# Attention output transposed by the DMA queue and added in the eviction, with the second token-mixing product row-tiled for two pairs at a time

## The chip, the cores and the metric

The kernel runs on one core of a Trainium2 chip. The metric is the device time of one execution in microseconds (us). Ratios are the mean time of one kernel's fast runs over the mean of the other's fast runs of the same rounds, with a 95% interval, so they are not quite the ratio of the medians that stand beside them. The change and the two groups of experiments (e1 to e4, e5 to e8) ran in separate rounds, so across them the ratios compare better than the medians.

## The reference, cut to what matters

```python
# B=8 batches, H=12 heads, S=448 rows, D=64; C=H*D=768; R=32; F=4*C
q_n, k_n = q / |q|, k / |k|                      # per row
attn = softmax(q_n @ k_n.T / tau)
x    = (attn @ v) -> [B, S, C]                   # heads side by side
h    = x.T @ U @ V                               # token mixing: U [S,R], V [R,S]
u    = x + h.T
out  = u + relu(u @ w_ch1) @ w_ch2               # channel mixing
```

Almost all arithmetic is in the two channel products. Attention and token mixing are done for two heads at a time (a "pair"; six pairs to a batch, 48 in all).

## The kernel before

For each pair, the attention output X (rows in four chunks of 128, 128 columns for two heads) is needed transposed, because the channel product contracts over columns. The kernel accumulates the transposed X (a product with the identity) and the low-rank term A V (A = X^T U, so the sum is u^T) in one PSUM bank, and then casts the bank to bf16.

```python
def step_A(b, p):                      # runs on PE and ScalarE
    X = X_of[(b, p)]
    ap = av_of[(b, p)][:, 384:512]
    for c in range(4):                 # A^T: U is 32 columns, padded to 128 with zeros
        nc.tensor.matmul(out=ap, lhsT=U_sb[:, c, :], rhs=X[:, c, :],
                         start=False, stop=(c == 3), skip_group_check=True)
    A = work.tile([128, 128], BF, name="A_sb", tag="A_sb", bufs=2)
    nc.scalar.copy(out=A, in_=ap)
    ...                                # [cut] up = one PSUM bank
    for c in range(4):                 # the transposed X, by the identity
        n = 128 if c < 3 else 64
        nc.tensor.matmul(out=up[:, c * 128:c * 128 + n], lhsT=X[:, c, :], rhs=ident[:, 0:n],
                         start=(c == 0), stop=False, skip_group_check=True)

def step_H(b, p):                      # the second product, 32 useful rows of 128
    nc.tensor.matmul(out=up, lhsT=A_of[(b, p)], rhs=V_sb,
                     start=False, stop=True, skip_group_check=True)
    ...
    nc.vector.tensor_copy(out=u_of(b)[:, p, 0:S], in_=up)
```

The channel products of the previous batch are a list of steps of about 1 us of PE work each (`fill`), which are dealt out between the attention steps of the current batch. From the third batch on, Q and K are transposed by the DMA queue (SP issues it) already. The weights are loaded early on GpSimd's own queue: `load_w1` in four parts, then `load_w2` in four.

Of the kernel before, what the change touches and what calls it, by code (L numbers as in the profile page):

```python
# [9 lines left out]
FP = mybir.dt.float32  # L10
BF = mybir.dt.bfloat16
# [11 lines left out]
def kernel(  # L23
# [16 lines left out]
    nc = tc.nc  # L40

    B, H, S, D = q.shape
    C = H * D
    R = moe_U.shape[-1]
    F = moe_w_ch1.shape[-1]
    NP = H // 2
# [5 lines left out]
    const = ctx.enter_context(tc.tile_pool(name="const", bufs=1))  # L52
    work = ctx.enter_context(tc.tile_pool(name="work", bufs=2))
    psum = ctx.enter_context(tc.tile_pool(name="psum", bufs=1, space=bass.MemoryType.PSUM))
# [29 lines left out]
    est = Estimate()  # L84
# [23 lines left out]
    for i in range(2):  # L108
        t = const.tile([128, 7, 512], BF, name=f"E{i}")
        nc.gpsimd.memset(t[:, :, S:512], 1.0)  # L110
        E.append(t)

    U_sb = const.tile([128, 4, 128], BF, name="U_sb")
    U_raw = const.tile([128, 4, R], FP, name="U_raw")
    V_raw = const.tile([R, S], FP, name="V_raw")
    V_sb = const.tile([128, S], BF, name="V_sb")
    w1_sb = const.tile([128, CC, F], BF, name="w1_sb")
    w2_sb = const.tile([128, NC, C], BF, name="w2_sb")
    uE = const.tile([128, CC, S], BF, name="uE")
# [3 lines left out]
    def load_mixer():  # L123
        nc.gpsimd.memset(U_sb, 0.0)
        nc.gpsimd.memset(V_sb, 0.0)
        nc.gpsimd.memset(U_raw[64:128, 3, :], 0.0)
        nc.gpsimd.dma_start(out=V_raw, in_=moe_V)
        nc.gpsimd.dma_start(out=U_raw[0:64, :, :], in_=moe_U[0:256].rearrange("(p c) r -> p c r", c=4))
        nc.gpsimd.dma_start(out=U_raw[64:128, 0:3, :], in_=moe_U[256:448].rearrange("(p c) r -> p c r", c=3))

    def place_mixer():
        lo = V_raw[:, 0:256].rearrange("r (p c) -> r c p", c=4)
        hi = V_raw[:, 256:448].rearrange("r (p c) -> r c p", c=3)
        body = V_sb[0:R, 0:384].rearrange("r (c p) -> r c p", p=128)
        nc.scalar.copy(out=U_sb[:, :, 0:R], in_=U_raw)
        nc.scalar.copy(out=body[:, :, 0:64], in_=lo[:, 0:3, :])
        nc.scalar.copy(out=body[:, :, 64:128], in_=hi)
        nc.scalar.copy(out=V_sb[0:R, 384:448], in_=lo[:, 3, :])

    def load_w1(f0, f1):  # L140
        nc.gpsimd.dma_start(out=w1_sb[:, :, f0:f1],
# [115 lines left out]
    def by_dma(n):  # L257

        return n >= 2 * NP
# [40 lines left out]
            est.pe(0.25)  # L300
            est.act(0.93)

    X_of, av_of, A_of, up_of = {}, {}, {}, {}

    def step_V(b, p, half):
        gi, j = group_of[(b, p)]
        vv = norm[gi][1]
        e = E[(b * NP + p) % 2]
        if half == 0:
            X_of[(b, p)] = work.tile([128, 4, 128], BF, name="X", tag="X", bufs=2)  # L310
        X = X_of[(b, p)]
        if b == 0 and half == 1:
            bank = psum.tile([128, 512], FP, name="mp", tag="ps_m", bufs=2)
        else:
            bank = psum.tile([128, 512], FP, name="av", tag="ps_av", bufs=1)
        av_of[(b, p)] = bank
        av = bank[:, 0:4 * (D + 1)].rearrange("p (i h d) -> p i h d", i=2, h=2)
        for i in range(2):
            ic = 2 * half + i
            nc.tensor.matmul(out=av[:, i, :, :], lhsT=e[:, 6, ic * 128:(ic + 1) * 128],  # L320
                             rhs=vv[:, 2 * j:2 * j + 2, 3, :],
                             start=(i == 0), stop=False, skip_group_check=True)
        for i in range(2):
            ic = 2 * half + i
            for h in range(2):
                for c in range(3):
                    nc.tensor.matmul(out=av[:, i, h, :],  # L327
                                     lhsT=e[:, 2 * c + h, ic * 128:(ic + 1) * 128],
                                     rhs=vv[:, 2 * j + h, c, :],
                                     start=False, stop=(i == 1 and h == 1 and c == 2),  # L330
                                     skip_group_check=True)
        rd = work.tile([128, 4, 1], FP, name="rd", tag="rd", bufs=4)
        nc.vector.reciprocal(out=rd, in_=av.rearrange("p i h d -> p (i h) d")[:, :, D:D + 1])  # L333
        nc.vector.tensor_mul(  # L334
            X[:, 2 * half:2 * half + 2, :].rearrange("p i (h d) -> p i h d", h=2),
            av[:, :, :, 0:D],
            rd.rearrange("p (i h) o -> p i h o", h=2).to_broadcast([128, 2, 2, D]))
        est.pe(0.52)
        est.dve(0.6)


    def u_of(b):
        return uE if b % 2 == 0 else uO

    def step_A(b, p):
        X = X_of[(b, p)]
        ap = av_of[(b, p)][:, 384:512]
        for c in range(4):
            nc.tensor.matmul(out=ap, lhsT=U_sb[:, c, :], rhs=X[:, c, :],  # L349
                             start=False, stop=(c == 3), skip_group_check=True)  # L350
        A = work.tile([128, 128], BF, name="A_sb", tag="A_sb", bufs=2)
        nc.scalar.copy(out=A, in_=ap)  # L352
        A_of[(b, p)] = A
        est.pe(0.44)
        est.act(0.3)
        if b == 0:
            up = psum.tile([128, S], FP, name="mp", tag="ps_m", bufs=2)
        else:
            up = psum.tile([128, S], FP, name="up", tag="ps_x", bufs=1)
        up_of[(b, p)] = up  # L360
        for c in range(4):
# [4 lines that stand above are left out]
    def step_H(b, p):  # L366
        up = up_of[(b, p)]
        nc.tensor.matmul(out=up, lhsT=A_of[(b, p)], rhs=V_sb,  # L368
                         start=False, stop=True, skip_group_check=True)
        est.pe(0.19)  # L370
        if b == 0:
            nc.scalar.copy(out=u_of(b)[:, p, 0:S], in_=up)
        else:
            nc.vector.tensor_copy(out=u_of(b)[:, p, 0:S], in_=up)  # L374
            est.dve(0.62)
        if b % 2 == 1 and p == NP - 1:
            nc.vector.tensor_copy(out=uO[:, :, S:512], in_=uE[:, :, 384:S])


# [77 lines left out]
    fill = []  # L457
# [3 lines left out]
    def f(n):  # L461
        for _ in range(n):
            fill.pop(0)()
# [21 lines left out]
    def T(n):  # L485
        step_T(*pairs[n])

    def Sc(n, *cs):
        step_S(*pairs[n], cs)

    def V(n, half):
        step_V(*pairs[n], half)

    def A(n):
        step_A(*pairs[n])

    def Hs(n):
        step_H(*pairs[n])
# [126 lines left out]
    def put(n, at, fn):  # L625
        after.setdefault((n, at), []).append(fn)
# [21 lines left out]
            put(m - 1, -1, lambda m=m: T(m))  # L648
            put(m - 1, 3, lambda m=m: T(m + 1))

    for n in range(NP, NPAIR + 1):
        b, p = pairs[n] if n < NPAIR else (B, 0)
        now, nxt = n < NPAIR, n + 1 < NPAIR
        done = n > NP
        for g in after.pop((n, -1), []):
            g()
        if n % 2 == 0:

            order = [
                (2, now and done and (lambda: Sc(n, 0, 1))),  # L660
                (2, done and (lambda: V(n - 1, 0))),
                (2, now and (lambda: Sc(n, 3))),
                (2, nxt and not by_dma(n + 1) and (lambda: T(n + 1))),
                (2, done and (lambda: V(n - 1, 1))),
                (1, done and (lambda: A(n - 1))),
                (1, nxt and (lambda: (Sc(n, 2), Sc(n + 1, 0)))),
                (1, done and (lambda: Hs(n - 1))),
            ]
        else:
            order = [  # L670
                (2, lambda: Sc(n, 1, 2)),
                (2, lambda: V(n - 1, 0)),
                (2, lambda: Sc(n, 3)),
                (2, lambda: V(n - 1, 1)),
                (2, nxt and not by_dma(n + 1) and (lambda: T(n + 1))),
                (2, lambda: A(n - 1)),
                (1, lambda: Hs(n - 1)),
            ]
        weights = [w if fn else 0 for w, fn in order]
        last = p == 0 and done  # L680
        left = NP - p + 0.85 if not last else 0.85
        nf = len(fill) if last else int(round(len(fill) / left))
        given = acc = 0
        for i, ((_, fn), w) in enumerate(zip(order, weights)):
            if fn:
                fn()
            for g in after.pop((n, i), []):
                g()
            acc += w
            want = nf * acc // sum(weights)  # L690
            f(min(want - given, len(fill)))
            given = want
        if last:
            f(len(fill))
            fill.extend(steps_m1(b - 1) + steps_m2(b - 1))
    f(len(fill))
    assert not after

# [34 lines left out]
```

## Time and profile before

| | before |
|---|---|
| time, median of 4 runs | 618.05 us (617.51 to 618.66) |
| span of the profiled run | 616.0 us |
| PE busy | 589.5 us (96%) |
| VectorE, ScalarE, GpSimd busy | 41%, 46%, 31% |

Busy shares are averages. What decides is whether PE ever waits, and the prediction below reads that from the list of PE's waits and its timeline. In the views PE is TensorE (matmuls) and PEld its weight loads, DVE is VectorE, ACT ScalarE, POOL GpSimd, and SP the engine that issues most DMAs; a bank is one part of PSUM, the memory that the matmuls write here, and to evict it is to copy it to SBUF, where the matmuls' operands lie. PEclk is the granted clock in tenths. Lines such as `302.76 0.36 PE L363 MATMUL ...` give start, duration, engine, source line, operation, tile written and tiles read, shape and count; what stands in brackets is the idle time just before and what ended it. Source lines of the changed kernel are numbered differently: L387, L414 become L439, L466 (channel products), L368 becomes L385 (second mixing product of the first two batches), L297 becomes L312 (row-tiled scores).

### The profile page before, as it was taken

The numbers are of one execution on the slowest core, as the hardware profiler recorded it, in microseconds if no ns is written. First come the engines' busy times: TensorE is split into PE (matmuls) and PEld (weight loads), VectorE is DVE, ScalarE is ACT, GpSimd is POOL, SyncE is SP. The second block draws the span as 40 slices with busy tenths as digits, with TensorE's granted clock in tenths as the row PEclk, the third lists the DMA queues.
The fourth block names the chain that finished last, engine by engine and source line by source line (L and its number), as shares of the span: only waits on it lengthen the run. The fifth ranks groups of instructions, "written<-read, shape, count | busy, mean of one in ns | idle before, by whom it ended". The sixth has DMA issues, their size and how long they took to land.

```text
span 616.0 us, 11649 instructions
## 1 busy us (share of the span) xinstructions
PE 589.5 (96%) x4872; PEld 346.3 (56%) x4872; DVE 249.5 (41%) x478; ACT 284.3 (46%) x519; POOL 190.2 (31%) x155
## 2 busy tenths in 40 slices
PE   1769999999999999999999999999999999999997
PEld 0445556655665555655566556565566555665564
DVE  5763665525325435335244454354352552110000
ACT  5775444455334555355442554354533455314310
POOL 7746274224044054043141351340431410000000
PEclk9998999999999999999999999999999999999999
DMA  7999995662074650562055641373135310110012
GB/s 187 214 230 223 233 216 133 173 150 36 10 166 116 151 125 1 138 167 52 7 134 134 160 100 39 63 174 91 35 95 99 69 24 12 27 37 17 1 51 53
DMA packets 89365, 63.80 MB, mean 104 GB/s; under 512 B 43120, under 2 KB 85664, under 8 KB 89312
## 3 DMA queue, kind: packets, MB, share of 16 engines
q1 hardware_dynamic: 82320, 52.60, 36.0%
q0 software_dynamic: 6688, 10.24, 9.2%
q8 instruction: 38, 0.62, 0.4%
q10 hardware_dynamic: 304, 0.21, 0.1%
q14 instruction: 15, 0.12, 0.1%
HBM read 52.02 MB, written 11.01 MB: 102 GB/s over the span
## 4 chain that ended last, share of the span: by engine, by line
PE 87%; DMA 8%; SPq 2%; POOL 1%; DVE 1%; ACT 1%; issue 0%; POOLq 0%; ACTq 0%
PE mp L414 36%; PE mp L387 32%; PE av L327 5%; PE sc L297 5%; DMA kst<-in_k_dram 5%; DMA vst<-in_v_dram 3%; PE av L320 2%; PE av L349 2%; PE mp L423 2%; PE up L363 1%; PE up L368 1%; PE sc L289 1%; POOL sq L215 1%; DMA qst<-in_q_dram 1%; SPq L182 1%; DVE ss L220 0%
## 5 line engine op out<-in xcount | busy, mean ns | idle before, releaser
L414 PE MATMUL mp<-w_sb,relu 128*128 128x384 bf16 x1344 | 245.1, 326 | 0.0
L414 PEld LDWEIGHTS <-relu 128*128 128x128 bf16 x1344 | 123.5, 98 | 84.8 <-issue 12.2
L387 PEld LDWEIGHTS <-w_sb 128*128 128x128 bf16 x1152 | 106.4, 98 | 100.9 <-issue 11.7
L244 POOL TENSOR_TENSOR qk<-kst,inv 128x512 bf16<-128x512 f32 x47 | 58.1, 1257 | 288.7 <-DVE rd L333 147.8
L391 ACT ACTIVATE relu<-mp 128x448 bf16<-128x448 f32 x155 | 84.2, 543 | 120.0 <-PE mp L387 119.9
L299 ACT ACTIVATE E<-sc 128x896 bf16<-128x896 f32 x144 | 124.6, 918 | 23.7 <-PE sc L297 23.7
L387 PE MATMUL mp<-uE,w_sb 128*128 128x448 bf16 x576 | 121.8, 353 | 0.0
L387 PE MATMUL mp<-uO,w_sb 128*128 128x448 bf16 x576 | 117.1, 353 | 0.0
L428 ACT COPY o_sb<-mp 128x384 f32<-128x384 f32 x55 | 26.3, 478 | 103.5 <-PE mp L423 102.9
L333 DVE RECIPROCAL rd<-av 128x4 f32<-128x4 f32 x90 | 15.6, 174 | 119.8 <-PE av L327 119.7
L244 DVE TENSOR_TENSOR qk<-qst,inv 128x512 bf16<-128x512 f32 x48 | 62.3, 1327 | 0.1
L220 DVE TENSOR_REDUCE ss<-sq 128x16 f32<-128x1024 f32 (+1 forms) x50 | 58.4, 1168 | 7.3 <-POOL sq L215 6.3
L215 POOL TENSOR_TENSOR sq<-kst 128x1024 f32<-128x1024 f32 x21 | 47.3, 2253 | 18.6 <-DMA kst<-in_k_dram 14.6
L327 PE MATMUL av<-v,E 128*128 128x65 bf16 x1080 | 49.4, 195 | 0.0
L297 PE MATMUL sc<-qkT 64*128 64x448 bf16 x288 | 42.0, 367 | 5.5 <-DVE qkT L276 3.6
L327 PEld LDWEIGHTS <-E 128*128 128x128 bf16 x1152 | 46.6, 99 | 0.0
L215 POOL TENSOR_TENSOR sq<-qst 128x1024 f32<-128x1024 f32 x23 | 45.7, 1987 | 2.6 <-DMA vst<-in_v_dram 2.6
L393 DVE TENSOR_SCALAR relu<-mp 128x448 bf16<-128x448 f32 x37 | 23.1, 623 | 49.2 <-PE mp L387 49.2
L334 DVE TENSOR_TENSOR X<-av,rd 128x256 bf16<-128x256 f32 x90 | 38.2, 425 | 3.1
L291 ACT ACTIVATE E<-sc 128x448 bf16<-128x448 f32 x48 | 26.1, 543 | 22.1 <-PE sc L289 22.1
L374 DVE CAST uO<-up 128x448 bf16<-128x448 f32 x24 | 14.9, 621 | 47.4 <-PE up L368 47.4
L352 ACT CAST A_sb<-av 128x128 bf16<-128x128 f32 x42 | 11.1, 263 | 40.4 <-PE av L349 40.4
(78 smaller groups left out, 332.8 us busy)
## 6 DMA issues: line engine op xcount, KB each, us to landing
out_dram<-o_sb SPq DMA_DIRECT2D x54, 192.0 KB, 2.7
w_sb<-in_moe_w_ch_dram POOLq DMA_DIRECT2D x8, 1152.0 KB, 18.6
qst<-in_q_dram SPq DMA_DIRECT2D x23, 256.0 KB, 4.1
vst<-in_v_dram SPq DMA_DIRECT2D x46, 128.0 KB, 2.9
kst<-in_k_dram SPq DMA_DIRECT2D x44, 128.0 KB, 3.7
qst<-in_q_dram SPq DMA_DIRECT2D x23, 192.0 KB, 4.6
vst<-in_v_dram SPq DMA_DIRECT2D x46, 96.0 KB, 2.7
kst<-in_k_dram SPq DMA_DIRECT2D x44, 96.0 KB, 3.4
```

Source lines behind the costliest of these rows:

```text
L215: nc.gpsimd.tensor_mul(sq[:, 0:self.nh * 4, :], self.flat(t), self.flat(t))
L220: nc.vector.reduce_sum(self.ss[:, j, 0:self.nh * 4], self.sq[j][:, 0:self.nh * 4, :], axis=AX.X)
L244: eng.tensor_mul(qks[self.s][:, j, i, :, :, :], t[:, 2 * j:2 * j + 2, :, :].rearrange("p h c d -> p c h d"), iv.unsqueeze(3).to_broadcast( ...
L291: nc.scalar.activation(out=e[:, 6, 0:S], in_=sc[:, 0, 0:S], func=AF.Exp)
L297: nc.tensor.matmul(out=sc[:, h, 0:S], lhsT=t[r, 1, c * 128:(c + 1) * 128], rhs=t[r, 0, 0:S], start=True, stop=True)
L299: nc.scalar.activation(out=e[:, 2 * c:2 * c + 2, 0:S], in_=sc[:, :, 0:S], func=AF.Exp)
L327: nc.tensor.matmul(out=av[:, i, h, :], lhsT=e[:, 2 * c + h, ic * 128:(ic + 1) * 128], rhs=vv[:, 2 * j + h, c, :], start=False, stop=(i == ...
L334: nc.vector.tensor_mul(X[:, 2 * half:2 * half + 2, :].rearrange("p i (h d) -> p i h d", h=2), av[:, :, :, 0:D], rd.rearrange("p (i h) o -> ...
L387: nc.tensor.matmul(out=mp, lhsT=w1_sb[:, cc, f * 128:(f + 1) * 128], rhs=u[:, cc, 0:S], start=(cc == 0), stop=(cc == CC - 1))
L391: nc.scalar.activation(out=relu[:, f, o:o + S], in_=mp, func=AF.Relu)
L414: nc.tensor.matmul(out=mp, lhsT=relu[:, f, r0:r0 + 128], rhs=w2_sb[:, f, half * HC:(half + 1) * HC], start=(f == 0), stop=False, skip_grou ...
L428: nc.scalar.copy(out=o[:, cols], in_=mp)
```

## The change

Intent: from the third batch on, take the identity products off PE. A DMA transpose makes X^T in SBUF, and the vector engine adds it while it evicts the low-rank term. The second product has only 32 useful rows, so two pairs share the array: one on rows 0 to 63, the other on rows 64 to 127. That needs a second copy of U's columns and V's rows at 64 to 95.

```diff
-    V_raw = const.tile([R, S], FP, name="V_raw")
+    V_raw = work.tile([128, S], FP, name="V_raw", tag="XT", bufs=2)
+    A_sb = [const.tile([128, 128], BF, name=f"A_sb{i}") for i in range(2)]
...
+    def load_twin():
+        nc.gpsimd.dma_start(out=V_raw[64:64 + R, :], in_=moe_V)
+
+    def place_twin():
+        nc.gpsimd.tensor_copy(out=U_sb[:, :, 64:64 + R], in_=U_raw)
+        place_v(nc.gpsimd.tensor_copy, 64)          # three copies into V_sb[64:96]
...
+    def step_XT(b, p):
+        t = work.tile([128, 4, 128], BF, name="XT", tag="XT", bufs=2)
+        XT_of[(b, p)] = t
+        nc.sync.dma_start_transpose(out=t, in_=X_of[(b, p)].rearrange("p c d -> p (c d)"))
+
+    def step_A2(b, p):                              # no identity products
+        ...
+        rows = slice(64 * (p % 2), 64 * (p % 2) + 64)
+        nc.scalar.copy(out=A_of[(b, p)][rows, :], in_=ap[rows, :])
+
+    def step_H2(b, p):                              # a couple: pairs p and p + 1
+        ups = (psum.tile([128, 512], FP, name="av", tag="ps_av", bufs=1),
+               psum.tile([128, 512], FP, name="up", tag="ps_x", bufs=1))
+        for i in range(2):
+            rows = slice(64 * i, 64 * i + 64)
+            nc.tensor.matmul(out=ups[i][:, 0:S], lhsT=A_of[(b, p)][rows, :], rhs=V_sb[rows, :],
+                             start=True, stop=True)
+        for i in range(2):
+            xt = XT_of.pop((b, p + i)).rearrange("p c r -> p (c r)")
+            nc.vector.tensor_add(u_of(b)[:, p + i, 0:S], ups[i][:, 0:S], xt[:, 0:S])
...
+    put(NP, 4, load_twin)          # seventh pair
+    put(NP + 2, 0, place_twin)     # ninth pair
...
-                (2, now and done and (lambda: Sc(n, 0, 1))),
+                    (2, lambda: Sc(n, 0, 1)),
...                                  # late pairs: couple behind a score block, then two fill steps
+        Sc(n, 1, 2)
+        if n - 3 >= FIRST2:
+            H2(n - 3)
+        ...
+        f(2)
+        spread(n, order, nf - 2, 1)
```

The cuts leave out the rearranged order of the late pairs and the smaller edits.

More of the change, by code (lines that the diff above doesn't have):

```diff
@@ L111 @@
         E.append(t)
+    U_raw = const.tile([128, 4, R], FP, name="U_raw")
     U_sb = const.tile([128, 4, 128], BF, name="U_sb")
-    U_raw = const.tile([128, 4, R], FP, name="U_raw")
-    V_raw = const.tile([R, S], FP, name="V_raw")
+    V_raw = work.tile([128, S], FP, name="V_raw", tag="XT", bufs=2)
+    A_sb = [const.tile([128, 128], BF, name=f"A_sb{i}") for i in range(2)]
     V_sb = const.tile([128, S], BF, name="V_sb")
@@ L125, in load_mixer, with place_v @@
         nc.gpsimd.memset(V_sb, 0.0)
+        for t in A_sb:
+            nc.gpsimd.memset(t[64:128, :], 0.0)
         nc.gpsimd.memset(U_raw[64:128, 3, :], 0.0)
-        nc.gpsimd.dma_start(out=V_raw, in_=moe_V)
+        nc.gpsimd.dma_start(out=V_raw[0:R, :], in_=moe_V)
         nc.gpsimd.dma_start(out=U_raw[0:64, :, :], in_=moe_U[0:256].rearrange("(p c) r -> p c r", c=4))
         nc.gpsimd.dma_start(out=U_raw[64:128, 0:3, :], in_=moe_U[256:448].rearrange("(p c) r -> p c r", c=3))
+    def place_v(copy, r0):
+        rows = slice(r0, r0 + R)
+        lo = V_raw[rows, 0:256].rearrange("r (p c) -> r c p", c=4)
+        hi = V_raw[rows, 256:448].rearrange("r (p c) -> r c p", c=3)
+        body = V_sb[rows, 0:384].rearrange("r (c p) -> r c p", p=128)
+        copy(out=body[:, :, 0:64], in_=lo[:, 0:3, :])
+        copy(out=body[:, :, 64:128], in_=hi)
+        copy(out=V_sb[rows, 384:448], in_=lo[:, 3, :])
     def place_mixer():
-        lo = V_raw[:, 0:256].rearrange("r (p c) -> r c p", c=4)
-        hi = V_raw[:, 256:448].rearrange("r (p c) -> r c p", c=3)
-        body = V_sb[0:R, 0:384].rearrange("r (c p) -> r c p", p=128)
         nc.scalar.copy(out=U_sb[:, :, 0:R], in_=U_raw)
-        nc.scalar.copy(out=body[:, :, 0:64], in_=lo[:, 0:3, :])
-        nc.scalar.copy(out=body[:, :, 64:128], in_=hi)
-        nc.scalar.copy(out=V_sb[0:R, 384:448], in_=lo[:, 3, :])
+        place_v(nc.scalar.copy, 0)
+    def load_twin():
[3 more added lines that the diff above has]
+        place_v(nc.gpsimd.tensor_copy, 64)
     def load_w1(f0, f1):
@@ L301, in step_S @@
             est.act(0.93)
-    X_of, av_of, A_of, up_of = {}, {}, {}, {}
+    X_of, av_of, A_of, up_of, XT_of = {}, {}, {}, {}, {}
     def step_V(b, p, half):
@@ L313, in step_V @@
             bank = psum.tile([128, 512], FP, name="mp", tag="ps_m", bufs=2)
+        elif half == 1 and by_dma(b * NP + p):
+            bank = psum.tile([128, 512], FP, name="up", tag="ps_x", bufs=1)
         else:
@@ L350, in step_A @@
                              start=False, stop=(c == 3), skip_group_check=True)
-        A = work.tile([128, 128], BF, name="A_sb", tag="A_sb", bufs=2)
-        nc.scalar.copy(out=A, in_=ap)
+        A = A_sb[p % 2]
+        nc.scalar.copy(out=A[0:64, :], in_=ap[0:64, :])
         A_of[(b, p)] = A
@@ L376, in step_H @@
         if b % 2 == 1 and p == NP - 1:
+            nc.vector.tensor_copy(out=uO[:, :, S:512], in_=uE[:, :, 384:S])
+    def step_XT(b, p):
[3 more added lines that the diff above has]
+    def step_A2(b, p):
+        X = X_of[(b, p)]
+        ap = av_of[(b, p)][:, 384:512]
+        for c in range(4):
+            nc.tensor.matmul(out=ap, lhsT=U_sb[:, c, :], rhs=X[:, c, :],
+                             start=False, stop=(c == 3), skip_group_check=True)
+        if p % 2 == 0:
+            A_of[(b, p)] = A_of[(b, p + 1)] = A_sb[(p // 2) % 2]
+        rows = slice(64 * (p % 2), 64 * (p % 2) + 64)
+        nc.scalar.copy(out=A_of[(b, p)][rows, :], in_=ap[rows, :])
+        est.pe(0.22)
+        est.act(0.3)
+    def step_H2(b, p):
[5 more added lines that the diff above has]
+                             start=True, stop=True)
+        est.pe(0.19)
+        for i in range(2):
+            xt = XT_of.pop((b, p + i)).rearrange("p c r -> p (c r)")
+            nc.vector.tensor_add(u_of(b)[:, p + i, 0:S], ups[i][:, 0:S], xt[:, 0:S])
+            est.dve(0.62)
+        if b % 2 == 1 and p == NP - 2:
             nc.vector.tensor_copy(out=uO[:, :, S:512], in_=uE[:, :, 384:S])
@@ L649, with spread @@
             put(m - 1, 3, lambda m=m: T(m + 1))
-    for n in range(NP, NPAIR + 1):
-        b, p = pairs[n] if n < NPAIR else (B, 0)
-        now, nxt = n < NPAIR, n + 1 < NPAIR
-        done = n > NP
-        for g in after.pop((n, -1), []):
-            g()
-        if n % 2 == 0:
-            order = [
-                (2, now and done and (lambda: Sc(n, 0, 1))),
-                (2, done and (lambda: V(n - 1, 0))),
-                (2, now and (lambda: Sc(n, 3))),
-                (2, nxt and not by_dma(n + 1) and (lambda: T(n + 1))),
-                (2, done and (lambda: V(n - 1, 1))),
-                (1, done and (lambda: A(n - 1))),
-                (1, nxt and (lambda: (Sc(n, 2), Sc(n + 1, 0)))),
-                (1, done and (lambda: Hs(n - 1))),
-            ]
-        else:
-            order = [
-                (2, lambda: Sc(n, 1, 2)),
-                (2, lambda: V(n - 1, 0)),
-                (2, lambda: Sc(n, 3)),
-                (2, lambda: V(n - 1, 1)),
-                (2, nxt and not by_dma(n + 1) and (lambda: T(n + 1))),
-                (2, lambda: A(n - 1)),
-                (1, lambda: Hs(n - 1)),
-            ]
-        weights = [w if fn else 0 for w, fn in order]
-        last = p == 0 and done
-        left = NP - p + 0.85 if not last else 0.85
-        nf = len(fill) if last else int(round(len(fill) / left))
+    put(NP, 4, load_twin)
+    put(NP + 2, 0, place_twin)
+    def spread(n, order, nf, first=0):
+        weights = [w if fn is not False else 0 for w, fn in order]
         given = acc = 0
@@ L686 @@
                 fn()
-            for g in after.pop((n, i), []):
+            for g in after.pop((n, i + first), []):
                 g()
@@ L692, with X2, A2, H2 @@
             given = want
-        if last:
+    FIRST2 = 2 * NP
+    KEEP = 3
+    for n in range(NP, NPAIR + 1):
+        b, p = pairs[n] if n < NPAIR else (B, 0)
+        now, nxt = n < NPAIR, n + 1 < NPAIR
+        done = n > NP
+        late = n > FIRST2
+        for g in after.pop((n, -1), []):
+            g()
+        if not late:
+            if n % 2 == 0:
+                order = [
+                    (2, lambda: Sc(n, 0, 1)),
+                    (2, done and (lambda: V(n - 1, 0))),
+                    (2, lambda: Sc(n, 3)),
+                    (2, not by_dma(n + 1) and (lambda: T(n + 1))),
+                    (2, done and (lambda: V(n - 1, 1))),
+                    (1, done and (lambda: A(n - 1))),
+                    (1, lambda: (Sc(n, 2), Sc(n + 1, 0))),
+                    (1, done and (lambda: Hs(n - 1))),
+                ]
+            else:
+                order = [
+                    (2, lambda: Sc(n, 1, 2)),
+                    (2, lambda: V(n - 1, 0)),
+                    (2, lambda: Sc(n, 3)),
+                    (2, lambda: V(n - 1, 1)),
+                    (2, not by_dma(n + 1) and (lambda: T(n + 1))),
+                    (2, lambda: A(n - 1)),
+                    (1, lambda: Hs(n - 1)),
+                ]
+            last = p == 0 and done
+            nf = len(fill) if last else int(round(len(fill) / (NP - p + 0.85)))
+            spread(n, order, nf)
+            if last:
+                f(len(fill))
+                fill.extend(steps_m1(b - 1) + steps_m2(b - 1))
+            continue
+        def X2(m):
+            step_XT(*pairs[m])
+        def A2(m):
+            step_A2(*pairs[m])
+        def H2(m):
+            step_H2(*pairs[m])
+        if n % 2 == 0:
+            order = [
+                (2, lambda: V(n - 1, 0)),
+                (2, now and (lambda: Sc(n, 0, 1))),
+                (2, lambda: (V(n - 1, 1), X2(n - 1))),
+                (2, lambda: A2(n - 1)),
+                (2, now and (lambda: Sc(n, 3))),
+                (2, nxt and (lambda: (Sc(n, 2), Sc(n + 1, 0)))),
+                (2, not now and (lambda: H2(n - 2))),
+            ]
+            nf = len(fill) if not now else int(round((len(fill) - KEEP) / (1 + (-p) % NP)))
+            spread(n, order, nf)
+            if not now:
+                f(len(fill))
+                fill.extend(steps_m1(b - 1) + steps_m2(b - 1))
+            continue
+        Sc(n, 1, 2)
+        if n - 3 >= FIRST2:
+            H2(n - 3)
+        for g in after.pop((n, 0), []):
+            g()
+        if p == 1 and n - 2 > FIRST2:
@@ L694 @@
             f(len(fill))
             fill.extend(steps_m1(b - 1) + steps_m2(b - 1))
+        order = [
+            (2, lambda: V(n - 1, 0)),
+            (2, lambda: Sc(n, 3)),
+            (2, lambda: (V(n - 1, 1), X2(n - 1))),
+            (2, lambda: A2(n - 1)),
+            (1, None),
+            (1, None),
+        ]
+        nf = int(round((len(fill) - KEEP) / (1 + (-p) % NP)))
+        f(2)
+        spread(n, order, nf - 2, 1)
     f(len(fill))
```

## The prediction

> **What bounds the kernel now.** I read the page's busy table, its slices and its chain, then the list of what PE waited for, then PE's timeline.
>
> ```profile
> PE 589.5 (96%) x4872; PEld 346.3 (56%) x4872; DVE 249.5 (41%) x478; ACT 284.3 (46%) x519; POOL 190.2 (31%) x155
> PE   1769999999999999999999999999999999999997
> PEclk9998999999999999999999999999999999999999
> PE 87%; DMA 8%; SPq 2%; POOL 1%; DVE 1%; ACT 1%; issue 0%; POOLq 0%; ACTq 0%
> ```
>
> PE is busy in every slice after the third, and 87% of the chain that ended last is PE. The list of PE's waits, summed, comes to about 22 us; the timeline puts all of them before 52 us, the last one at 51.63. From there to the end PE never stands still, so a microsecond of PE work removed later comes off the end, and a new wait of PE, wherever it lies, goes on top. Two vector engines at 41% and 46% leave room. To price PE work I take starts, not busy times (matmuls overlap): from the start of one row to that of the next.
>
> ```profile
> 302.54 0.39 PE L349 MATMUL av<-X,U_sb 128*128 128x128 bf16 x4
> 302.76 0.36 PE L363 MATMUL up<-ident,X 128*128 128x128 bf16 x4
> 302.95 2.11 PE L414 MATMUL mp<-w_sb,relu 128*128 128x384 bf16 x12
> 304.90 0.33 PE L423 MATMUL mp<-ident,uO 128*128 128x128 bf16 x3
> 305.07 0.35 PE L368 MATMUL up<-V_sb,A_sb 128*128 128x448 bf16 x1
> 305.26 1.14 PE L414 MATMUL mp<-w_sb,relu 128*128 128x384 bf16 x6
> 306.33 0.55 PE L297 MATMUL sc<-qkT 64*128 64x448 bf16 x4
> 306.82 1.15 PE L414 MATMUL mp<-w_sb,relu 128*128 128x384 bf16 x6
> 307.80 0.28 PE L320 MATMUL av<-v,E 128*128 128x130 bf16 x2
> ```
>
> Here the four identity products (L363) hold PE for 302.95 - 302.76 = 0.19 us, the second mixing product (L368) for 0.19. Six L414 matmuls take 0.98 (306.82 to 307.80), but the six ahead of the row-tiled scores (L297) take 1.07 (305.26 to 306.33): 0.09 to enter 64-row tiling. The four score matmuls take 0.49. A block of two, in the timeline at 38.35, takes 0.30. So a concurrent pair costs 0.195, and leaving the mode the remaining 0.10.
>
> **What the skill says.** "TensorEngine Tiling (Array Packing)", Tiling Modes, Key Properties: a change of tiling mode drains TensorE. The trace agrees: about 0.095 us each way. "TensorE: Matmul & The Clock Gate", Part 3, The mechanism: matmuls in different row groups run together, starts some 4 ns apart. It agrees: two 448-column matmuls for 0.195 us, where one alone takes 0.19. Same page, Part 1: a window of about 3.4 us without enough work halves the clock. It agrees in this trace after far less than 3.4 us of idleness:
>
> ```profile
> 46.05 0.38 PE L349 MATMUL mp<-X,U_sb 128*128 128x128 bf16 x4 [1.95 <-DVE X L334]
> ...
> 46.47 0.28 PE L320 MATMUL av<-v,E 128*128 128x130 bf16 x2
> ...
> 47.53 0.42 PE L320 MATMUL mp<-v,E 128*128 128x130 bf16 x2
> ...
> 50.25 0.55 PE L297 MATMUL sc<-qkT 64*128 64x448 bf16 x4
> 50.74 0.36 PE L368 MATMUL mp<-V_sb,A_sb 128*128 128x448 bf16 x1
> 51.63 0.35 PE L289 MATMUL sc<-qkT 128*128 128x448 bf16 x1 [0.53 <-ACT E L299]
> ```
>
> After an idle 1.95 us the same L320 pair goes from 0.28 to 0.42, and the clock digit of that slice is 8: one window at half speed. Same page, Architectural detail: GpSimd takes its instructions strictly in order. POOL's timeline agrees (no later group overtakes one that waits for a load).
>
> **The change, part by part** (36 pairs, 18 couples, from the third batch on):
> - Removed from PE: 36 x (0.19 + 0.19) = 13.7 us.
> - Added to PE: 18 concurrent pairs x 0.195 = 3.5 us. The order of the changed program shows 17 of them directly behind a score block, already in the mode; the last stands alone and pays 0.19 for the switch. Net so far 13.7 - 3.5 - 0.2 = 10.0 us less.
> - Transposes: 36 more on SP's queue. The 36 there take 1.28 us to issue and 3.2 to land. The transpose is queued with the second half of a pair's values, and its couple's product comes at the latest two thirds of a pair (a pair takes about 12 us: 500 us over 42) later, some 7 us against about 0.8 + 3.2. Hidden.
> - Vector: the 36 casts (0.62 us) become adds. The L334 multiply of 256 columns from the same kind of source takes 0.42, so the cost goes by column and a 448-column add should be 0.62 as well. Each couple takes both single banks, but two fill steps (2 us) stand before the next product into the first bank, and its add ends some 1 us after the couple. Hidden, with about 1 us to spare.
> - Second halves of values now go to another bank than first halves: one wait less, where there was none.
> - An accident: at the seventh pair the changed code issues score chunks 0 and 1 that the prologue has already issued. The order shows 292 row-tiled score matmuls for 288 and 146 wide exponentials for 144. The repeat comes just after 50.9 us, when both score buffers wait for exponentials (0.92 each; that is the 0.53 above). Buffers come free at 51.63 and about 52.55, so fill starts at about 52.9 in place of 51.8: 1.2 us more with L289.
> - **The second copy of V** (for rows 64 to 95) is the costly part:
>
> Its load is issued on POOL's queue behind the weight loads, and POOL's copies of it (the first new POOL instructions in the order) write the rows of the tiles that every mixing product reads. The order with its waits shows that at the ninth pair the first product waits for POOL's copy of U, and the second for the copies of V, which wait for the load. When does it land? The group of the second weight's loads:
>
> ```profile
> L145 POOL DMA_DIRECT2D w_sb<-in_moe_w_ch_dram x4: 826/836/871, 50.2 to 52.7; - x4
> DMA to landing us min/median/max: 12.1/22.5/33.2
> ```
>
> They are issued from 50.2 to 52.7 and land after 12 to 33 us, the last at 52.7 + 33.2 = 85.9. They land one behind the other, as the earlier loads of this queue do, so I take a load issued after them (at about 61) to land at about 86.2. The product that needs it, in PE's timeline of the kernel before, and POOL's last work ahead of it:
>
> ```profile
> 81.91 0.35 PE L368 MATMUL up<-V_sb,A_sb 128*128 128x448 bf16 x1
> ```
> ```profile
> 77.87 1.89 POOL L215 TENSOR_TENSOR sq<-qst 128x1024 f32<-128x1024 f32 x1
> ```
>
> POOL copies U from 79.8, in time for the first product at 79.77 + 1.2. The second product would start at 81.91 + 1.2 = 83.1. The V copies start at 86.2; at some 1 ns a column (1.04 us for 1024 columns in the L252 casts), with 448 columns in three pieces, they end at about 87.1. So PE waits about 4.0 us, all of it new: the score repeat shortens it, since it came first. In an idle stretch of this length the clock should halve for one window of 3.4 us, as after 46 us; at half speed that is another 1.7. Together 5.7 us more. POOL's own delay (its next key scaling moves from 82.84 to about 88) reaches a transpose that PE runs at 89.23 + 6.9, so it costs nothing further.
>
> Sum: -10.0 + 1.2 + 5.7 = -3.1 us. I add 0.4 for small waits in the rearranged pairs (vector engine in order behind 1.2 to 1.4 us reductions and scalings). 618.2 - 2.7 = 615.5; as the wait may be shorter than I make it, I put the middle at 614.8.
>
> **Rivals.**
> (a) The second V lands early, its few rows passing the weights. For it: it is 56 KB, the weights 1152 KB each. Against: the landings of that queue are strictly one after another. Then 618.2 - 10.0 + 1.2 + 0.4 = 609.8.
> (b) The vector engine, in order, becomes the bound in the late pairs: its adds wait for a transpose held up in SP's queue behind ten loads of 0.6 us each, and PE waits for the bank. For it: each bank is single, and SP issues about 6.5 us of loads per two pairs. Against: the transposes are queued half a pair before those loads. If each of 18 couples lost 0.4 us, it would take 7 us more: 622.
> (c) All is hidden and the repeat costs nothing: 608.2. Against: PE had no idle time after 52 us that could swallow the repeat. More than that cannot be gained, since only 10.0 us of PE work goes; 2% would be 12.4 us.
> (d) The transposes slow the loads. Against: the DMA engines work at under half load after 103 us, and loads are issued two groups ahead.
>
> **Range and chances.** The mechanism of the V copy I hold for likely (some 8 in 10), its size for uncertain (2 to 7 us with the clock). Its absence gives 609 to 611, a full wait with late small waits 617 to 618. So 610.0 to 618.0 should hold it 8 times in 10. Faster by over 2% (under 605.9) would need more than all removed work: 0.01. Slower by over 2% (over 630.6) needs rival (b) at twice its size: 0.02.
>
> **What would show it.** After: the identity product and the single second product should be gone from the late pairs; the couple of products should start 4 ns apart and hold PE for 0.2 us; PE's list of waits should have one wait of about 4 us of the second product for POOL near 83 us, and a clock digit below 9 in the slice that holds 88 us; a wait of 0.5 to 1 us for an exponential near 51 to 53; no wait over 0.3 us after 100 us. The prediction is wrong if that POOL wait is missing (rival a), if waits for the adds or for the values come back in each pair (rival b), or if the late pairs gain other than 10 us.

## The result, and the profile after

| | before | after |
|---|---|---|
| time, median of 4 runs | 618.05 us (617.51 to 618.66) | 615.79 us (614.10 to 616.20) |
| ratio | | 0.9958 (0.9936 to 0.9980) |
| span of the profiled run | 616.0 us | 614.4 us |
| PE busy | 589.5 us | 580.0 us |

PE is busy for 9.5 us less, and the time falls by 2.3. From the page of the changed kernel, PE's share by slice and the granted clock:

```profile
PE   1768969999999999999999999999999999999997
PEclk9999979999999999999999999999999999999999
```

The sixth slice (77 to 92 us) was full before and shows 6 tenths now; its clock is 7 tenths. From the list of PE's waits of the changed kernel (waited for; us in total, times, longest):

```profile
PE up L385 <- POOL V_sb L142: 5.6, 1, 5.6
```

PE's timeline around it:

```profile
81.30 1.31 PE L439 MATMUL mp<-uE,w_sb 128*128 128x448 bf16 x6
88.21 0.53 PE L385 MATMUL up<-V_sb,A_sb 128*128 128x448 bf16 x1 [5.61 <-POOL V_sb L142]
88.53 2.44 PE L439 MATMUL mp<-uE,w_sb 128*128 128x448 bf16 x6
90.91 0.93 PE L312 MATMUL sc<-qkT 64*128 64x448 bf16 x4
```

The product stands still for 5.61 us, and the six channel matmuls behind it take 2.44 us where six take 1.31 just before: the clock is halved. The trace's clock record has it at one half from 85.98 to 92.81 us, two windows of 3.41 us, of which 4.60 us (from 88.21) hold PE work; at most half of that, 2.3 us, is lost. Experiment e4 below puts it at 2.2.

GpSimd's timeline of the changed kernel says why:

```profile
61.24 0.56 POOL L149 DMA_DIRECT2D V_raw<-in_moe_V_dram  x1
...
79.21 0.29 POOL L152 CAST U_sb<-U_raw 128x128 bf16<-128x128 f32 x1
87.03 0.51 POOL L140 CAST V_sb<-V_raw 32x192 bf16<-32x192 f32 x1 [7.53 <-DMA V_raw<-in_moe_V_dram]
87.49 0.43 POOL L141 CAST V_sb<-V_raw 32x192 bf16<-32x192 f32 x1
87.87 0.28 POOL L142 CAST V_sb<-V_raw 32x64 bf16<-32x64 f32 x1
```

The load is issued at 61.24, behind the second weight, and takes 25.6 us to land: at 86.89, 0.47 us after the last of the four parts of that weight (62.94, 70.72, 78.38 and 86.42). The first load of V, of the same 56 KB and with no weight ahead of it, lands 4.1 us after its issue. The three copies of the second V end at 88.15, and PE's product starts at 88.21, which is 6.30 us later than before (81.91). With the 2.2 of the half clock that makes 8.5.

The late pairs do what was intended. PE's timeline of the changed kernel, a couple behind its score block:

```profile
320.05 0.55 PE L312 MATMUL sc<-qkT 64*128 64x448 bf16 x4
320.43 0.35 PE L421 MATMUL av<-V_sb,A_sb 64*128 64x448 bf16 x1
320.44 0.35 PE L421 MATMUL up<-V_sb,A_sb 64*128 64x448 bf16 x1
320.72 2.12 PE L466 MATMUL mp<-w_sb,relu 128*128 128x384 bf16 x12
```

The two products start together (in all 18 couples the second starts 3 or 4 ns after the first). From the block's start to the next fill step it is 0.67 us, against 0.49 for a score block alone: the couple costs 0.18. The adds take 0.62 us, and no wait for them is in the list of PE's waits. The transposes of X (36, a median of 2.4 us from issue to landing) are hidden.

To split the time into the stretch before the change takes hold and the late pairs, compare where the channel product of the second and of the last batch starts on PE. Before:

```profile
123.30 1.31 PE L387 MATMUL mp<-uO,w_sb 128*128 128x448 bf16 x6
...
551.89 1.30 PE L387 MATMUL mp<-uO,w_sb 128*128 128x448 bf16 x6
```

After:

```profile
131.75 1.50 PE L439 MATMUL mp<-uO,w_sb 128*128 128x448 bf16 x7
...
550.03 1.68 PE L439 MATMUL mp<-uO,w_sb 128*128 128x448 bf16 x8
```

At the first of these points the changed kernel is 131.75 - 123.30 = 8.45 us behind, as the sum above says. From there on it takes 418.28 us for what took 428.59, so it gains 10.31. The net is 1.86 us, which is nearly the difference of the spans.

### The profile page after: what moved, and what is told of

Read it like the earlier page. It is cut to its first block, busy times and chain, and to the rows that moved or that the text cites. A ratio compares the mean times of both kernels' runs of the same rounds, so it can differ in the third digit from the quotient of the medians.

```text
span 614.4 us, 11493 instructions
## 1 busy us (share of the span) xinstructions
PE 580.0 (94%) x4732; PEld 335.8 (55%) x4732; DVE 238.1 (39%) x474; ACT 288.7 (47%) x525; POOL 193.9 (32%) x162
## 4 chain that ended last, share of the span: by engine, by line
PE 85%; DMA 9%; SPq 2%; issue 1%; POOL 1%; DVE 1%; ACT 0%; POOLq 0%
PE mp L466 36%; PE mp L439 32%; PE sc L312 5%; DMA vst<-in_v_dram 4%; DMA qst<-in_q_dram 3%; PE av L344 3%; DMA kst<-in_k_dram 2%; PE up L344 2%; PE mp L475 2%; PE up L407 1%; PE sc L304 1%; PE av L337 1%; PE up L337 1%; SPq L199 1%; POOL sq L230 1%
## 5 line engine op out<-in xcount | busy, mean ns | idle before, releaser
L259 POOL TENSOR_TENSOR qk<-kst,inv 128x512 bf16<-128x512 f32 x47 | 67.7, 1459 | 282.9 <-DVE inv L253 269.0
L443 ACT ACTIVATE relu<-mp 128x448 bf16<-128x448 f32 x164 | 89.3, 545 | 126.0 <-PE mp L439 126.0
L350 DVE RECIPROCAL rd<-av 128x4 f32<-128x4 f32 x54 | 9.7, 180 | 132.6 <-PE av L344 132.6
L259 DVE TENSOR_TENSOR qk<-qst,inv 128x512 bf16<-128x512 f32 x48 | 52.4, 1122 | 0.8
L230 POOL TENSOR_TENSOR sq<-kst 128x1024 f32<-128x1024 f32 x21 | 41.0, 1953 | 15.0 <-DMA kst<-in_k_dram 11.3
L344 PE MATMUL av<-v,E 128*128 128x65 bf16 x648 | 29.6, 194 | 0.0
L445 DVE TENSOR_SCALAR relu<-mp 128x448 bf16<-128x448 f32 x28 | 17.4, 621 | 29.3 <-PE mp L439 28.8
L350 DVE RECIPROCAL rd<-up 128x4 f32<-128x4 f32 x36 | 6.5, 182 | 53.5 <-PE up L344 53.2
L267 POOL CAST v<-vst 128x1024 bf16<-128x1024 f32 (+1 forms) x25 | 26.0, 1041 | 2.5 <-DMA vst<-in_v_dram 2.5
L312 PEld LDWEIGHTS <-qkT 64*128 64x128 bf16 x292 | 9.3, 95 | 29.7 <-issue 21.6
```

The costliest lines, as they stand in the source:

```text
L230: nc.gpsimd.tensor_mul(sq[:, 0:self.nh * 4, :], self.flat(t), self.flat(t))
L259: eng.tensor_mul(qks[self.s][:, j, i, :, :, :], t[:, 2 * j:2 * j + 2, :, :].rearrange("p h c d -> p c h d"), iv.unsqueeze(3).to_broadcast( ...
L267: nc.gpsimd.tensor_copy(out=self.flat(v65[self.s])[:, :, 0:D], in_=self.flat(vst[self.s]))
L312: nc.tensor.matmul(out=sc[:, h, 0:S], lhsT=t[r, 1, c * 128:(c + 1) * 128], rhs=t[r, 0, 0:S], start=True, stop=True)
L344: nc.tensor.matmul(out=av[:, i, h, :], lhsT=e[:, 2 * c + h, ic * 128:(ic + 1) * 128], rhs=vv[:, 2 * j + h, c, :], start=False, stop=(i == ...
L443: nc.scalar.activation(out=relu[:, f, o:o + S], in_=mp, func=AF.Relu)
```

## The experiments

Theory: the late pairs give about 10 us; the late second copy of V takes most of it back, by PE's wait and by the half clock that follows; the repeated score chunks at the seventh pair cost about 1 us, but only where that wait does not hide them. Rivals: another wait stands behind this one; the load or the copies hurt by themselves; the half clock has another cause; running two products side by side gains nothing.

All eight kernels gave correct results. Times are medians of 4 or 5 runs; the kernel before had a median of 618.07 us in the rounds of the first four and 617.78 us in those of the last four.

| run | what it is | median us | ratio to before |
|---|---|---|---|
| the change | | 615.79 | 0.9958 |
| e1_twin_early | second V loaded early | 608.83 | 0.9852 (0.9837 to 0.9867) |
| e2_no_repeat | without the repeated chunks | 615.63 | 0.9966 (0.9953 to 0.9978) |
| e3_early_no_repeat | both | 607.96 | 0.9833 (0.9820 to 0.9847) |
| e4_busy_pe | PE kept busy through the wait | 614.81 | 0.9945 (0.9933 to 0.9958) |
| e5_copies_later | late load, later copies | 609.17 | 0.9853 (0.9838 to 0.9868) |
| e6_no_row_tiling | transposes alone | 611.18 | 0.9887 (0.9873 to 0.9900) |
| e7_twin_in_before | late second V in the kernel before | 625.87 | 1.0126 (1.0112 to 1.0140) |
| e8_no_gap | no fill between a couple and the next product | 617.73 | 0.9996 (0.9984 to 1.0009) |

### The load moved ahead of the weights (e1)

```diff
         nc.gpsimd.dma_start(out=V_raw[0:R, :], in_=moe_V)
+        load_twin()
...
-    put(NP, 4, load_twin)
```

> The second copy of V is loaded right behind the first one, ahead of the weights; nothing else changes. Theory (the late load makes PE wait 5.6 us, and the half clock after it costs another 2.3): no wait of L385 for POOL near 83 us, no clock digit below 9 after 60 us, and 615.8 - 7.9 = 607.9 us (607.2 to 608.8). Rival (another wait stands right behind this one, for instance for the third group's keys, which POOL scales late): the wait moves to another line and the time stays above 612.

Measured: 608.83 us, 7.0 us less than the change (6.6 by the ratios), just outside the range given. No wait of PE for GpSimd's copies is left, and from 52 us on the longest wait of PE is 0.23 us. PE and clock by slice:

```profile
PE   1668999999999999999999999999999999999997
PEclk9999999999999999999999999999999999999999
```

The wait was real and had nothing behind it. The profiled spans differ by more, 614.4 - 606.6 = 7.8, but the profiled run of the change was the slowest of its four (616.2) and that of e1 the fastest (608.42).

### The repeated chunks taken out, alone and together with the early load (e2, e3)

```diff
-                    (2, lambda: Sc(n, 0, 1)),
+                    (2, done and (lambda: Sc(n, 0, 1))),
```

> The repeated score chunks of the seventh pair are taken out; V's second copy stays late. Theory (PE must wait until 88.2 us for POOL in any case, so work ahead of that is free): the wait for POOL grows by about 1.1 us to 6.7 and the time stays at 615.8 (615.2 to 616.4). Rival (the repeat costs its own 1.2 us, as the prediction's sum has it with a wait of fixed size): 614.6.

> Both: early load and no repeat. Theory: now the repeat is no longer hidden by the wait, so this is 1.1 us faster than the early load alone: 606.8 us (606.2 to 607.7), about 11.2 us less than the kernel before, of which 10.0 is removed PE work. Rival (the repeat costs nothing, or the late pairs give back part of the work): equal to the early load alone within 0.3 us, or no more than 9 us less than before.

Measured: alone 615.63 us, no change. With the early load 607.96 us, which misses the range given by 0.3. The ratios 0.9852 and 0.9833 put the gain of the second edit at 0.0019 x 618, about 1.2 us, the medians at 0.9; the intervals overlap, but every run of e3 (607.21 to 608.04) is faster than every run of e1 (608.42 to 609.13). The same edit is worth nothing in one kernel and about 1 us in the other. In the first, PE's product starts when the copies are done, whatever PE did before:

```profile
87.99 0.53 PE L385 MATMUL up<-V_sb,A_sb 128*128 128x448 bf16 x1 [5.30 <-POOL V_sb L142]
```

That is at 87.99 us, against 88.21 with the repeat. One detail of the expectation missed: the wait was to grow to 6.7 us and is 5.3, since PE's first channel product started late in this run (52.35 us, against 51.50 in e3), behind start-up waits for VectorE's copies of qkT that sum to 4.6 us, against 3.4 in e3. So in these two profiled runs PE came to the wait at the same moment (82.69 and 82.60 us): that the wait hides the repeat is shown by the times, not by these two traces.

e3 is the fastest kernel: 10.1 us less than the kernel before.

### PE kept busy through the wait (e4)

```diff
+    def busy(count):
+        if count:
+            mp = psum.tile([128, S], FP, name="mp", tag="ps_m", bufs=2)
+            for i in range(count):
+                nc.tensor.matmul(out=mp, lhsT=w1_sb[:, 0, 0:128], rhs=uE[:, 0, 0:S],
+                                 start=(i == 0), stop=(i == count - 1))
...
-                    (1, done and (lambda: Hs(n - 1))),
+                    (1, done and (lambda: (busy(28 if n == NP + 2 else 0), Hs(n - 1)))),
```

> 28 matmuls of 448 columns whose result nobody reads (about 5.3 us) are put on PE just ahead of the product that waits for the second copy of V; all else as in the changed kernel. Theory (the idle wait halves the clock for two windows): the wait for POOL shrinks from 5.6 to 0.3 us, it starts at the same 88.2 us, the clock stays full, and the time falls by 2.3 us to 613.5, though PE has more to do. Rival (the half clock has another cause or costs nothing): 615.8, or more if the added work delays something.

Measured: 614.81 us, 1.0 less than the change by the medians and 0.0013 x 618 = 0.8 by the ratios, whose intervals overlap; so less than the 2.3 expected, and by the times alone not clear. The profiled run shows what happened, in PE's timeline:

```profile
82.71 5.46 PE L724 MATMUL mp<-uE,w_sb 128*128 128x448 bf16 x28
88.07 0.35 PE L385 MATMUL up<-V_sb,A_sb 128*128 128x448 bf16 x1
88.25 1.30 PE L439 MATMUL mp<-uE,w_sb 128*128 128x448 bf16 x6
```

With 28 useless matmuls, the product starts at the same time (88.07), six channel matmuls behind it take 1.30 us and not 2.44, and no clock digit falls. From the start of the product to the first matmul of the second weight it takes 94.56 - 88.07 = 6.49 us, against 96.86 - 88.21 = 8.65 in the change: the half clock cost 2.2 us there, and the stretch without work brought it about. In e2's profiled run, with a wait of nearly the same length, only one window is halved (87.67 to 91.09, 3.1 us of work, so 1.55 lost). How much of a stretch of work falls into halved windows depends on where the windows lie, so 2.2 is one run's value. Of the runs that were not profiled the record has the mean clock: 0.994 in all four of the change, 0.997 to 0.999 in e4's five. A halved window is worth 3.41 / 2 / 614 = 0.003, so e4's runs have one or two windows less, but the mean does not say how much PE work lay in them. Why the timed runs gain only 0.8 to 1.0 us stays open; the profiled spans, 2.3 us apart, are of the change's slowest run and e4's fastest.

### Late load, later copies (e5)

```diff
-    put(NP + 2, 0, place_twin)
+    put(NP + 5, 0, place_twin)
```

> The load of the second V stays late, behind the weights; only POOL's copies of it move from the ninth pair to the twelfth (ahead of it POOL has its squares; the first product that reads the tiles after them comes at about 110 us). Theory (the cost lies only in reading, at the ninth pair, what lands at 87 us): no wait for POOL near 83 us, and the time of the early load, 608.8 us (608.0 to 609.8). Rival (the load itself disturbs, or the copies on POOL delay the products wherever they stand): above 611.

Measured: 609.17 us, the same as the early load (ratios 0.9853 and 0.9852). GpSimd copies from 107.98 to 109.46 us, behind its squares, and PE does not wait for it. So neither the late load nor the copies cost anything; only the place of the first reader does.

### The transposes without the row tiling (e6)

```diff
-        if p % 2 == 0:
-            A_of[(b, p)] = A_of[(b, p + 1)] = A_sb[(p // 2) % 2]
-        rows = slice(64 * (p % 2), 64 * (p % 2) + 64)
+        A_of[(b, p)] = A_sb[p % 2]
+        rows = slice(0, 64)
...
-            nc.tensor.matmul(out=ups[i][:, 0:S], lhsT=A_of[(b, p)][rows, :], rhs=V_sb[rows, :],
+            nc.tensor.matmul(out=ups[i][:, 0:S], lhsT=A_of[(b, p + i)], rhs=V_sb,
```

(and without the second copies and the repeat)

> The transposes by DMA and the add stay, but the two second products of a couple run one after the other on all 128 rows (the lower half of A is zero), so that no second copy of U and V is needed; without the repeat. Compared with the kernel that has the early load and no repeat (607.96 us). Theory: 18 couples lose the overlap of one product each, 18 x (0.378 - 0.186) = 3.4 us, less 0.2 for one mode switch: 611.2 us (610.6 to 611.9), so that the transposes alone give about 7 of the 10 us. Rival (side by side is not worth it, because the couple drains the array or waits for its banks either way): 608.

Measured: 611.18 us. Against e3 the ratios differ by 0.9887 - 0.9833 = 0.0054, or 3.3 us for 18 couples. PE's timeline of e6, a couple:

```profile
313.99 0.36 PE L419 MATMUL av<-V_sb,A_sb 128*128 128x448 bf16 x1
314.19 0.35 PE L419 MATMUL up<-V_sb,A_sb 128*128 128x448 bf16 x1
314.38 0.81 PE L464 MATMUL mp<-w_sb,relu 128*128 128x384 bf16 x4
```

The two products take 0.39 us in sequence, against 0.18 to 0.19 side by side. So the transposes give some 7 us and the row tiling 3.3. This variant needs no second V. A first draft of it with two more A tiles did not build: the pool wanted 29.125 KB per partition and 28.875 were left.

### The late second V alone, in the kernel before (e7)

The kernel before with `load_twin` and the three copies of V at the same two places. The rows written multiply zeros of A, so the result stays right.

> The kernel before, with only the late load of the second V and POOL's three copies of it at the ninth pair (rows that multiply zeros there, so the result is right). Theory: the second product that started at 81.91 us waits for the copies, which end at 88.1: 6.2 us, and the half clock after it costs 1.5 to 2.3 more, so 618.1 + 8.1 = 626.2 us (625.3 to 627.2). Rival (the wait hurts only together with the new arrangement of the late pairs): 618 to 620.

Measured: 625.87 us, a ratio of 1.0126, that is 7.8 us more. PE's timeline:

```profile
88.09 0.53 PE L378 MATMUL up<-V_sb,A_sb 128*128 128x448 bf16 x1 [5.38 <-POOL V_sb L138]
```

The wait was to be 6.2 us and is 5.4, since PE comes to it 0.8 us later in this run; the product starts 88.09 - 81.91 = 6.2 us later than before, as expected, and the clock digit of the sixth slice is 7. The loss belongs to the second copy of V, and not to the new arrangement.

### No fill between a couple and the next product (e8)

On the kernel e3:

```diff
-        f(2)
-        spread(n, order, nf - 2, 1)
+        spread(n, order, nf, 1)
```

> On the kernel with the early load and without the repeat (607.96 us): the two steps of fill that stand between a couple's products and the next product into the first of their banks are moved behind it. Theory (those two steps, 2 us, hide the vector engine's add, which ends about 1.1 us after the couple starts): PE waits for the add about 0.8 us in each of 17 pairs, so 14 us more, 622 us (616 to 625), and the list of PE's waits shows the first product of values waiting for the add. Rival (the bank comes free anyway): 608.

Measured: 617.73 us, within the range given, and 0.9996 - 0.9833 = 0.0163, or 10.1 us, more than e3. One place in PE's timeline of e8:

```profile
316.25 0.35 PE L422 MATMUL av<-V_sb,A_sb 64*128 64x448 bf16 x1
316.25 0.35 PE L422 MATMUL up<-V_sb,A_sb 64*128 64x448 bf16 x1
317.32 0.29 PE L338 MATMUL av<-v,E 128*128 128x130 bf16 x2 [0.71 <-DVE uE L427]
```

The next product into the couple's first bank starts 1.07 us after the couple; with fill in between, PE would have gone on about 0.28 us after it. So 0.79 us is lost each time. The list of PE's waits has 12 such waits, and not 17: at the second pair of a batch three steps of fill that were kept back still follow the couple. 12 x 0.79 = 9.5 us, which is nearly all of the 10.1. So the wait was sized right and the number of places was not; the wide range held the result. The two steps of fill are what makes the vector engine's add free.

## Why the prediction was right

It gave 614.8 us (610.0 to 618.0), and 615.79 was measured. The mechanism was right in each of its parts: work leaves PE, the transposes and adds are hidden, and one new wait for the second V, with a half clock behind it, takes most of the gain back. That the number came so near is in part luck. The stretch up to the second batch was sized 1.55 us too small; the late pairs gained 0.31 more than worked out, and the 0.4 added for small waits did not come, which cancels nearly half of that. The last step, from 615.5 down to 614.8 because the wait might be shorter, went the wrong way: the wait was longer. Point by point:

- **Less PE work, 10.0 us.** Measured 10.31 in the late pairs. A couple costs 0.18, a little less than the 0.195 that it was sized at. "TensorEngine Tiling (Array Packing)", Tiling Modes, Key Properties, says that a mode switch drains the array; the couple behind a score block pays for no switch of its own, and these 0.18 us show it.
- **Transposes and adds hidden.** Right: the adds take the predicted 0.62 us, the transposes land sooner than the 3.2 us assumed (2.4), and no wait for either is in the list. e8 confirms the spare time: the add releases the bank 1.07 us after the couple, and two steps of fill last about 2 us.
- **The wait for the second V, 4.0 us.** The mechanism was right, the size too small: 5.61. PE came at 82.6 us and not 83.1; the copies began at 87.03 and not 86.2; they took 1.12 us and not 0.9. The Trainium skill's page "DMA: Bandwidth & Descriptors", Two DMAs through the same engine are not ordered, says that descriptors within one queue of one DMA engine start in order, and promises no order of landing. In this trace the loads of that queue also land in order: the 56 KB issued at 61.24 behind the weights landed 25.6 us later, just after the last weight. GpSimd's own work behind the copies held nothing up: after 95 us PE's list of waits is empty.
- **The half clock, 1.7 us for one window.** It came, but over two windows in the profiled run: 2.2 us. The mean clock of the other three runs, 0.994 as well, fits two halved windows but does not say where they lie. The prediction reads the page as a window without enough work, where the page's table says idle; the list at the end shows that the traces fit the prediction's reading better.
- **The repeat, 1.2 us.** Its size was about right (0.9 to 1.2), as e1 and e3 show, and its sign came: waits of 0.53 and 0.44 us for exponentials before 50.94 and 51.75 us. In the change itself it costs nothing that e2 could measure, because the wait ends at a fixed moment. The prediction's sum had this in it: it counted the repeat and then took the wait from a later arrival of PE. The two together were put at 6.9 us and measured 8.45.
- **Rivals.** (a), an early landing, is refuted by the landing; its time of 609.8 is close to e1's 608.83, where the early landing is built. (b) and (d) did not happen: there is no late wait. (c) had 608.2 with the repeat hidden, and e3, without the repeat, measured 607.96.

## What to carry to other kernels

Where the trace shows that PE never stands still, work taken from it comes off the time: here 10.0 us were worked out and 10.31 measured in the late pairs. So look for what the change adds elsewhere: here a 56 KB load, queued behind four weight loads of 1152 KB each and read at the ninth pair, gave back some 7 of these 10 us. Before adding a read of a constant, ask what else is in its queue and who reads it first; load it before the bulk, or move the first reader. A wait that ends at a fixed moment hides whatever stands ahead of it on the waiting engine, so such small costs show only once the wait is gone.

## What the Trainium skill lacked or had wrong

- "TensorE: Matmul & The Clock Gate", Part 1 and the table of why this matters, puts the fall to half clock after an idle window of about 3.4 us. Here PE need not be idle for so long. In the kernel before the clock record has one half from 46.68 to 50.09 us; in the 3.41 us ahead of it PE was busy for 1.46 us, and its longest gap was 1.95. Over the ten profiled runs the 3.41 us just ahead of such a fall held up to 1.73 us of PE work (e5), while four runs with 1.58 to 1.69 us at the same place (e8, e4, e7, e1) saw no fall. So the limit lies near half of the window here, and it is not sharp.
- The same page, Back-to-back issue gap, gives a sustained 81 ns for matmuls of 128 columns and 131 ns for 512, each with its weight load, and N/2.4 + 2.5 ns for an isolated one of N columns. Here six of 448 columns take 1.14 us (190 ns each), twelve of 384 take 1.95 us (162 ns each), and four of 128 take 0.22 us (55 ns each), every one with its own weights. That is the formula for the isolated one (189, 162.5 and 56 ns, worked out from it), and not the sustained figures.
- "TensorEngine Tiling (Array Packing)", Key Properties, names the drain at a mode switch without a cost. Here it is, by the differences of starts in the prediction, about 0.09 us in and 0.10 out, and two 448-column products on 64 rows each take 0.18 us against 0.39 in sequence.
- For a transpose by DMA into SBUF the skill has one time, for 128 by 128 ("VectorE: DVE Perf Modes", The three transpose paths, 1309 ns), and none for larger tiles or for the issue. Here one of 128 rows by 512 columns in bf16 lands 2.4 us after its issue, one of 128 by 1024 after 3.2 (medians), and SP needs 1.2 to 1.3 us to issue either.
